# Batch 0's first quarter of q as fp32 on ScalarE's DMA queue, packed by heads and transposed in 128x128 blocks

## The chip, the cores and the metric

The kernel runs on one core of a Trainium2 chip. The time is the device time of one execution in microseconds (us). The kernel before took 399.16 us as the median of five runs (399.06 to 399.82). Beside these runs there is one profiled execution, from which all rows of a profile come.

A core has five engines, each with its own queue of instructions that it works through in order: TensorE (PE; its weight loads are shown as PEld), VectorE (DVE), ScalarE (ACT), GpSimd (POOL) and SyncE (SP). Transfers are issued from SP's and ACT's queues (the profile calls them hardware queues) and from POOL's (the software queue), and are carried by 16 DMA engines. Only transfers on POOL's queue change the type from fp32 to bf16 on the way here.

## The reference, cut to what matters

Attention with projected keys and values, then a feed-forward layer with a maximum over three matrices:

```python
k_proj = np.einsum('ks,bhsd->bhkd', E, k)       # E, F: 64 x 1024
v_proj = np.einsum('ks,bhsd->bhkd', F, v)       # q, k, v: 8 batches, 8 heads, 1024, 64
scores = scale * np.matmul(q, k_proj.transpose(0, 1, 3, 2))
attn = softmax(scores)                          # written out in the reference
x = np.matmul(attn, v_proj)                     # heads side by side: 8192 x 512
h = np.maximum(np.maximum(x @ w1, x @ w2), x @ w3)   # 512 x 768 each
out = h @ w_out                                 # 768 x 512
```

All inputs and the output are fp32; the kernel works in bf16 with fp32 sums.

## The kernel before, in words

The program works batch by batch, and each batch in two chunks of 512 rows. A row index s is split as s = p * 8 + si, with p the partition; a chunk is four of the eight si. For one chunk the up part (L687 and `up`, L738) multiplies x by the three weight matrices, 128 columns (jt, of six) at a time, and takes the maximum. The down part (L788) multiplies by w_out and stores. The attention of the next batch is put between these matmuls by a hand-written plan (L830 on). The instructions of each engine run in the order in which the program writes them; a small model of the clocks (`clock`, `free`, L67) only decides which of the eight PSUM banks a step takes, and `at(us)` (L588) sets that model's time by hand.

Batch 0 has a head of its own, L652 to L682, and this is where the change lies. Its transfers are all issued at the start:

- SP loads E and F (L148, L149) as fp32, 64 rows each, into `ef_f`.
- POOL loads, in this order: q for heads 0 to 3 and the first four si (`load_q(LO, ...)`, L167), k for heads 0 to 3 (L168), q for heads 4 to 7 and the first four si (L169), k for heads 4 to 7 (L170), two pieces of v (L171, L172), then after `ident` has been made weights, the two other pieces of v, more weights, the rest of q (L194) and w_out.

The head computes with the first chunk of q alone (`C0 = (0, SPC)`):

- `idle(n, w)` (L563) are filler matmuls on zeros; with `warm_f` in fp32, with `warm` in bf16.
- `turn_ef` (L570) casts E and F to bf16 (`ef_b`, half on DVE, half on ACT), transposes them in eight 128x128 blocks on TensorE (L578), and copies the result to `efT`, half on DVE, half on ACT.
- `q_duo(0)` (L633, with `heads_q`, L361) transposes q for two pairs of heads: 16 transposes of 64 columns each, since a head has 64 numbers and the heads of a pair lie apart in `q_t`; DVE copies the result to `qT`.
- A DVE copy (L656) writes the F columns of `efT` a second time.
- `k_duo(u)` (L593) projects k for four heads with `efT` (L596), `kt_duo(u)` transposes the result (L609), `scores` (L219) multiplies it with `qT`, `exps`, `z` and `x` make the softmax and the first x, `v_pair` (L622) projects v.
- `up_first` (L702) starts the first chunk's up matmuls (L689) while the later heads' attention is still under way. Its first maxima lie in `hs`, a fp32 tile of 128 x 6 x 512 that exists once; its first writes are the copies at L725.

For the second chunk of batch 0, `pack_q` (L373) copies q so that the two heads of a pair lie side by side (tile `q_p`), on ACT, and `qp` (L386) transposes whole 128x128 blocks of it (L393).

```python
copy("s", q_pk[b][:, g, lo:lo + nsi].rearrange("p si h d -> p h si d"),
     qkv[b][0][:, 2 * g:2 * g + 2, lo:lo + nsi], (), 0.58)
```

Every plain copy is recorded at the line of the helper `copy` (L102), so in the profile such rows are told apart by their tiles.

Of the kernel before, what the change touches and what calls it, by code (L numbers as in the profile page):

```python
# [8 lines left out]
FP32 = mybir.dt.float32  # L9
BF16 = mybir.dt.bfloat16  # L10
# [5 lines left out]
def kernel(  # L16
# [13 lines left out]
    nc = tc.nc  # L30

    B, H, S, D = q.shape
# [5 lines left out]
    P = 128  # L38
    HALF = 64
    SI = 8  # L40
    NCT = DM // P
    NJT = DF // P
    NPAIR = H // 2
    CHUNK = 512
    NCHUNK = S // CHUNK
    SPC = SI // NCHUNK
# [24 lines left out]
    def deal(ns):  # L71
        clock["pe"] = max(clock["pe"], *(free[n] for n in ns))
        for n in ns:
            assert free[n] < OPEN
            free[n] = OPEN

    def two():
        n = min(range(0, 8, 2), key=lambda n: max(free[n:n + 2]))
        deal((n, n + 1))
        return psum_t[:, n:n + 2, :], (n, n + 1)  # L80

    def bank():
        n = min(range(8), key=lambda n: free[n])
        deal((n,))
        return psum_t[:, n, :], (n,)

    def pe(dt, wait=0.0):
        clock["pe"] = max(clock["pe"], wait) + dt
        return clock["pe"]

    def runs(eng, ready, dt, ns=()):
        if eng in clock:
            clock[eng] = max(clock[eng], ready + 0.06) + dt
            for n in ns:
                free[n] = clock[eng]
            return clock[eng]
        return ready + dt
# [3 lines left out]
    def copy(eng, o, i, ns=(), dt=0.65):  # L101
        done = {  # L102
            "v": nc.vector.tensor_copy, "s": nc.scalar.copy, "g": nc.gpsimd.tensor_copy
        }[eng](out=o, in_=i)
        runs(eng, clock["pe"] if ns else 0.0, dt, ns)
        return done
# [10 lines left out]
    def view(src, b):  # L117
        return src[b].rearrange("h (p si) d -> p h si d", si=SI)


    ident = const.tile([P, P], BF16, name="ident")
# [9 lines left out]
    qkv, qTs, kpTs, vps, pTs, zis, xTs = {}, {}, {}, {}, {}, {}, {}  # L131
# [19 lines left out]
    def load_kv(i, heads):  # L151
        nc.gpsimd.dma_start(  # L152
            out=qkv[0][i][:, heads], in_=view((q, k, v)[i], 0)[:, heads]
        )

    def load_q(heads, sis):
        nc.gpsimd.dma_start(  # L157
            out=q_t[:, heads, sis], in_=view(q, 0)[:, heads, sis]
        )
# [4 lines left out]

    LO, HI, ALL = slice(0, H // 2), slice(H // 2, H), slice(0, H)
    V2, V3 = slice(4, 6), slice(6, 8)
    load_q(LO, slice(0, SPC))  # L167
    load_kv(1, LO)  # L168
    load_q(HI, slice(0, SPC))  # L169
    load_kv(1, HI)  # L170
# [56 lines left out]
    def exps(b, g, lo, nsi, sc):  # L227
        t, ns, ready = sc
        pTs[b, g, lo] = att.tile([P, 2, CHUNK], BF16, name="pT", bufs=6)[:, :, 0:nsi * HALF]
        nc.scalar.activation(out=pTs[b, g, lo], in_=t, func=AF.Exp, scale=scale)  # L230
        runs("s", ready, 0.17 + nsi * 0.107, ns)
# [14 lines left out]
    def sums(b, g, lo, nsi):  # L246
        return pair_mm(b, g, lo, nsi, lambda rows, hp: ones[rows])
# [48 lines left out]
    def invert(b, g, lo, nsi, z):  # L296
        t, ns, ready = z
        zl = att.tile([P, 2, CHUNK], FP32, name="zl", bufs=1)[:, :, 0:nsi * HALF]
        nc.scalar.activation(out=zl, in_=t, func=AF.Ln)  # L299
        runs("s", ready, 0.17 + nsi * 0.107, ns)  # L300
        if nsi == SI:
            zi = zi_all(b)[:, g]
        else:
            zi = att.tile([P, 2, CHUNK // 2], FP32, name="zi0", bufs=4)
        nc.scalar.activation(out=zi, in_=zl, func=AF.Exp, scale=-1.0)  # L305
        zis[b, g, lo] = zi, runs("s", ready, 0.17 + nsi * 0.107)

    def values(b, g, lo, nsi):
        if b not in xTs:
            xTs[b] = att.tile([P, NCT, SI, P], BF16, name="xT")  # L310
        return pair_mm(b, g, lo, nsi, lambda rows, hp: vps[b][rows, 2 * g + hp, :])

    def scale_x(b, g, lo, nsi, av):
        t, ns, ready = av
        zi, when = zis.pop((b, g, lo))
        nc.vector.tensor_tensor(  # L316
            out=xTs[b][:, g, lo:lo + nsi, :].rearrange("a (c s) p -> a c (s p)", c=2),
            in0=t, in1=zi, op=ALU.mult,
        )
        runs("v", max(ready, when), 0.17 + nsi * 0.13, ns)  # L320
# [3 lines left out]
    def run_later():  # L324
        for f in later:
            f()
        later.clear()
# [33 lines left out]
    def heads_q(b, g, sis, t):  # L361
        for i, si in enumerate(sis):
            for hp in range(2):
                nc.tensor.transpose(
                    out=t[hp * HALF:(hp + 1) * HALF, i * P:(i + 1) * P],
                    in_=qkv[b][0][:, 2 * g + hp, si, :],
                    identity=ident,
                )
        pe(0.08 * len(sis))

    q_pk = {}

    def pack_q(b, gs, lo, nsi):  # L373


        def f():
            if b not in q_pk:
                q_pk[b] = att.tile([P, NPAIR, SI, 2, D], BF16, name="q_p", bufs=1)
            for g in gs:
                copy(  # L380
                    "s", q_pk[b][:, g, lo:lo + nsi].rearrange("p si h d -> p h si d"),
                    qkv[b][0][:, 2 * g:2 * g + 2, lo:lo + nsi], (), 0.58,
                )
        return f

# [184 lines left out]
    def turn_ef():  # L570
        for i in range(2):
            cols = slice(i * S // 2, (i + 1) * S // 2)
            copy("vs"[i], ef_b[:, cols], ef_f[:, cols])
        t, ns = two()
        t = t.bitcast(BF16)[:, 0]
        src = ef_b.rearrange("k (p si) -> k p si", si=SI)
        for si in range(SI):
            nc.tensor.transpose(  # L578
                out=t[:, si * P:(si + 1) * P], in_=src[:, :, si], identity=ident
            )  # L580
        pe(0.6)
        for i in range(2):
            copy(
                "vs"[i], efT[:, 4 * i:4 * i + 4, 0:P],
                t[:, i * CHUNK:(i + 1) * CHUNK].rearrange("p (si x) -> p si x", x=P), ns,
            )

    def at(us):  # L588
        clock["pe"] = max(clock["pe"], us)
# [43 lines left out]
    def q_duo(u):  # L633
        t, ns = bank()
        t = t.bitcast(BF16)
        for gg in range(2):
            heads_q(0, 2 * u + gg, range(SPC), t[:, gg * CHUNK:(gg + 1) * CHUNK])
        o = qTs[0].rearrange("a (g si) p -> a g si p", si=SI)
        copy(
            "v", o[:, 2 * u:2 * u + 2, 0:SPC, :],  # L640
            t.rearrange("a (g si p) -> a g si p", si=SPC, p=P), ns, 0.7,
        )

    C0 = (0, SPC)

    def z(g):
        invert(0, g, *C0, sums(0, g, *C0))

    def x(g):
        scale_x(0, g, *C0, values(0, g, *C0))  # L650

    idle(3, warm_f)  # L652
    at(6.3)
    turn_ef()
    q_duo(0)
    copy("v", efT[:, :, P:P + KP], efT[:, :, KP:P])  # L656
    idle(1, warm_f)
    at(9.0)
# [4 lines left out]
    for g in (0, 1):  # L663
        exps(0, g, *C0, scores(0, g, *C0))
    at(10.6)
# [12 lines left out]
    for g in (2, 3):  # L678
        exps(0, g, *C0, scores(0, g, *C0))
    at(16.1)  # L680
    v_pair(1)
    at(17.4)  # L682

    ffn_sb = ctx.enter_context(tc.tile_pool(name="ffn_sb", bufs=2))
    hTs = {}

    def up_mm(h, i, b, ch, jt, cts, first=0, last=NCT - 1):  # L687
# [14 lines left out]
    def up_first(work):  # L702


        def then(key):
            run_later()
            for f in work.get(key, []):
                f()

        hs = ffn_sb.tile([P, NJT, CHUNK], FP32, name="hs", bufs=1)  # L710
        hTs[0, 0] = ffn_sb.tile([P, NJT, CHUNK], BF16, name="hT")
        jts = range(NJT)
        h = {}
        for ct, js in (
            (0, range(0, 4)), (1, range(0, 4)), (0, range(4, 6)), (1, range(4, 6)),
            (2, jts), (3, jts),
        ):
            for jt in js:
                if jt not in h:
                    t, ns = two()  # L720
                    for n in (0, 1):
                        h[jt + n] = t[:, n], ns[n:n + 1]
                up_mm(h[jt][0], 0, 0, 0, jt, (ct,))
                if ct == NCT - 1:
                    copy("sv"[jt % 2], hs[:, jt], *h[jt])  # L725
                then((0, ct, jt))
        for i in (1, 2):
            h = []
            for jt in jts:
                h.append(bank())  # L730
                up_mm(h[jt][0], i, 0, 0, jt, range(NCT // 2))
                then((i, "a", jt))
            for jt in jts:
                up_mm(h[jt][0], i, 0, 0, jt, range(NCT // 2, NCT))
                most(hs[:, jt] if i == 1 else hTs[0, 0][:, jt, :], *h[jt], hs[:, jt])
                then((i, jt))
# [154 lines left out]
    for b in range(B):  # L891
        p = plan(b)
# [63 lines left out]
```

## Time and profile before

| | |
|---|---|
| median of five runs | 399.16 us |
| profiled execution, its own time | 399.06 us |
| its span in the profile | 397.3 us |
| granted TensorE clock | 1.0 |
| DMA, mean over the span | 167 GB/s |
| POOL issues: first q quarter, first k half | at 1.26 and 2.14 us |
| issue to landing: E, F | 3.2 and 4.3 us |
| issue to landing: the two first quarters of q | 5.3 and 8.3 us |
| first k projection (L596), first matmul | 9.97 us |
| first up matmul (L689) | 17.65 us |

Times in the profile are counted from the start of the span. A row of the timeline gives the start, the duration, the engine, the line, the operation with the tile it writes and the tile it reads, and in brackets how long the engine was idle before it and what ended that idle time. "x8" behind a row means that eight instructions are merged. The view of the transfers counts packets, the pieces in which a queue moves its data, for each queue in a window, and gives the busy share of the 16 DMA engines, which may pass 1 where an engine has several pieces in flight. The page of the whole execution gives the busy time of each engine, and the chain of work that ended last, followed back from the end.

### The profile page before, as it was taken

What the parts mean: (1) busy time and instruction counts of PE and PEld (TensorE: products, weight loads), DVE (VectorE), ACT (ScalarE), POOL (GpSimd) and SP (SyncE); (2) the same over time, 40 slices, a digit from 0 to 9 for tenths busy, and PEclk for the clock granted to TensorE, in tenths of its full rate; (3) what the DMA queues carried; (4) which work ended last, traced back from release to release, by engine and by line L of the source; (5) the groups of instructions that cost most, each with busy time, mean ns of one, the idle gap of its engine ahead of it and who ended that gap; (6) DMA issues with size and microseconds to landing.
All of it is one profiled execution on the core that took longest, in us unless ns stands there. A gap on an engine that the chain in (4) does not pass through costs nothing.

```text
span 397.3 us, 5598 instructions
## 1 busy us (share of the span) xinstructions
PE 387.2 (97%) x2196; PEld 173.6 (44%) x2238; DVE 202.3 (51%) x309; ACT 152.1 (38%) x236; POOL 34.5 (9%) x49
## 2 busy tenths in 40 slices
PE   7999999999999999999999999999999999999996
PEld 3544443453445445444444444444444444444443
DVE  3348756751764525645374544845266443745251
ACT  2534638527222552263323532245323533132322
POOL 7440011000400200200002000200000000000000
PEclk9999999999999999999999999999999999999999
DMA  9999999987899998999979979696971138020202
GB/s 151 205 205 208 205 247 148 248 149 159 229 181 260 157 224 200 229 184 202 213 208 149 245 164 272 101 241 117 221 207 42 63 89 235 2 106 0 107 0 106
DMA packets 67338, 66.29 MB, mean 167 GB/s; under 512 B 31504, under 2 KB 59792, under 8 KB 67312
## 3 DMA queue, kind: packets, MB, share of 16 engines
q0 software_dynamic: 29104, 30.41, 47.4%
q1 hardware_dynamic: 38064, 35.46, 34.6%
q8 instruction: 17, 0.28, 0.3%
q10 hardware_dynamic: 144, 0.07, 0.1%
q14 instruction: 9, 0.07, 0.1%
HBM read 69.73 MB, written 16.97 MB: 218 GB/s over the span
## 4 chain that ended last, share of the span: by engine, by line
PE 90%; DMA 3%; DVE 2%; POOL 2%; issue 1%; ACT 1%; DVEq 0%; ACTq 0%; POOLq 0%
PE banks L689 61%; PE banks L797 20%; DMA v_t<-in_v_dram 3%; PE banks L239 2%; PE banks L353 2%; PE banks L219 2%; PE banks L528 1%; PE banks L264 1%; DVE xT L316 1%; DVE m L758 1%; ACT zi_all L305 1%; ACT zl L299 1%; DVE hT L699 0%; POOL k_t L152 0%; POOL q_t L157 0%
## 5 line engine op out<-in xcount | busy, mean ns | idle before, releaser
L689 PE MATMUL banks<-xT,w_sb 128*128 128x512 bf16 x1125 | 255.2, 379 | 1.9 <-DVE xT L316 0.3
L689 PEld LDWEIGHTS <-w_sb 128*128 128x128 bf16 x1152 | 110.2, 98 | 136.7 <-issue 8.5
L758 DVE TENSOR_TENSOR m<-banks,h1s 128x512 f32<-128x512 f32 x90 | 62.1, 690 | 131.3 <-ACT h1s L754 88.6
L754 ACT COPY h1s<-banks 128x512 f32<-128x512 f32 x90 | 52.7, 586 | 119.5 <-PE banks L689 119.5
L797 PE MATMUL banks<-wout_sb,hT 128*128 128x512 bf16 x364 | 85.5, 380 | 1.0 <-issue 0.3
L699 DVE TENSOR_TENSOR hT<-banks,m 128x512 bf16<-128x512 f32 x90 | 62.3, 692 | 9.7 <-DVE m L758 0.5
L797 PEld LDWEIGHTS <-hT 128*128 128x128 bf16 x378 | 35.3, 98 | 48.3 <-issue 6.1
L102 ACT COPY o_sb<-banks 128x512 f32<-128x512 f32 (+2 forms) x57 | 32.9, 578 | 58.3 <-PE banks L797 50.6
L316 DVE TENSOR_TENSOR xT<-banks,zi_all 128x1024 bf16<-128x1024 f32 x28 | 33.2, 1220 | 12.8 <-PE banks L239 8.2
L230 ACT ACTIVATE pT<-banks 128x1024 bf16<-128x1024 f32 (+1 forms) x32 | 30.3, 976 | 16.0 <-PE banks L219 16.0
L201 POOL DMA_DIRECT2D q_t<-in_q_dram x7 | 6.1, 877 | 196.7 <-DMA qT<-q_p 60.7
L102 ACT CAST vp<-banks 64x256 bf16<-64x256 f32 (+1 forms) x11 | 4.7, 424 | 20.5 <-DVE kp L102 11.2
L102 DVE CAST vp<-banks 64x256 bf16<-64x256 f32 (+2 forms) x15 | 6.7, 445 | 10.1 <-ACT vp L102 7.3
L239 PE MATMUL banks<-pT,vp 64*64 64x512 bf16 (+1 forms) x128 | 10.3, 375 | 0.5 <-DVE vp L102 0.2
L102 DVE COPY q_p<-q_t 128x1024 bf16<-128x1024 bf16 x26 | 9.7, 433 | 0.2 <-DMA q_t<-in_q_dram 0.2
L219 PE MATMUL banks<-qT,kpT 64*64 64x512 bf16 (+1 forms) x128 | 9.7, 372 | 0.0
L102 DVE CAST kp<-banks 128x256 bf16<-128x256 f32 (+2 forms) x9 | 4.6, 509 | 8.7 <-PE banks L528 3.5
L102 DVE COPY o_sb<-banks 128x512 f32<-128x512 f32 (+1 forms) x9 | 5.6, 640 | 5.4 <-PE banks L777 4.5
L567 PE MATMUL banks<-warm_f 128*128 128x512 f32 x8 | 6.4, 946 | 1.5 <-DVE warm_f L175 1.5
L299 ACT ACTIVATE zl<-banks 128x512 f32<-128x512 f32 (+1 forms) x8 | 6.5, 811 | 2.9 <-PE banks L239 2.7
L353 PEld LDWEIGHTS <-efT 128*64 128x64 bf16 x128 | 6.6, 110 | 2.1 <-issue 2.1
L201 POOL DMA_DIRECT2D v_t<-in_v_dram x7 | 6.5, 931 | 1.0 <-PE banks L689 1.0
(76 smaller groups left out, 136.3 us busy)
## 6 DMA issues: line engine op xcount, KB each, us to landing
out_dram<-o_sb SPq DMA_DIRECT2D x30, 512.0 KB, 3.8
zi_all<-zd SPq DMA_DIRECT2D x20, 512.0 KB, 7.9
q_t<-in_q_dram POOLq DMA_DIRECT2D x7, 1024.0 KB, 10.7
k_t<-in_k_dram POOLq DMA_DIRECT2D x7, 1024.0 KB, 17.1
v_t<-in_v_dram POOLq DMA_DIRECT2D x7, 1024.0 KB, 21.6
zi_all<-zd POOLq DMA_DIRECT2D x4, 512.0 KB, 7.6
w_sb<-in_moe_w_dram POOLq DMA_DIRECT2D x4, 384.0 KB, 11.1
k_t<-in_k_dram POOLq DMA_DIRECT2D x2, 512.0 KB, 9.0
```

Of the source, the lines that this page charges most:

```text
L102: done = {"v": nc.vector.tensor_copy, "s": nc.scalar.copy, "g": nc.gpsimd.tensor_copy}[eng](out=o, in_=i)
L201: dma = nc.gpsimd.dma_start(out=tiles[i], in_=view((q, k, v)[i], b))
L219: nc.tensor.matmul(out=t[c * HALF:(c + 1) * HALF, hp, 0:n * P], lhsT=k_pair(b, g)[rows], rhs=qTs[b][rows, at:at + n, :], start=True, stop= ...
L230: nc.scalar.activation(out=pTs[b, g, lo], in_=t, func=AF.Exp, scale=scale)
L239: nc.tensor.matmul(out=t[hp * HALF:(hp + 1) * HALF, c, 0:nsi * HALF], lhsT=w(rows, hp), rhs=p[rows, hp, :], start=True, stop=True,)
L316: nc.vector.tensor_tensor(out=xTs[b][:, g, lo:lo + nsi, :].rearrange("a (c s) p -> a c (s p)", c=2), in0=t, in1=zi, op=ALU.mult,)
L353: nc.tensor.matmul(out=t[hh * HALF:(hh + 1) * HALF, 0:width], lhsT=efT[:, si, (kv - 1) * KP:kv * KP], rhs=qkv[b][kv][:, heads[hh], si, :], ...
L689: nc.tensor.matmul(out=h, lhsT=w_sb[i][:, ct, jt * P:(jt + 1) * P], rhs=xTs[b][:, ct, ch * SPC:(ch + 1) * SPC, :], start=(ct == first), st ...
L699: nc.vector.tensor_tensor(out=o, in0=h, in1=other, op=ALU.max)
L754: nc.scalar.copy(out=h1s, in_=h[0][0])
L758: nc.vector.tensor_tensor(out=m12, in0=h[1][0], in1=h1s, op=ALU.max)
L797: nc.tensor.matmul(out=o_ps, lhsT=hTs[b, ch][:, jt, tt * P:(tt + 1) * P], rhs=wout_sb[:, jt, :], start=(jt == 0), stop=(jt == NJT - 1),)
```

## The change

The q quarter of heads 0 to 3 and the first four si leaves POOL's queue. It is loaded on ACT's queue, as fp32 without a change of type, into the first two of the six parts of `hs`; for this the pool of `hs` is opened earlier and `hs` is allocated in the head. The DMA stands ahead of ACT's table load (L174) in the program. Right behind the two casts of E and F, `pack_q` casts and packs this quarter by pairs of heads into `q_p`: pair 0 on DVE, pair 1 on ACT. In place of `q_duo(0)`, a new `q_first` transposes eight 128x128 blocks of `q_p`, and DVE copies the result to `qT`. The second quarter (heads 4 to 7) still comes over POOL and is still turned by `q_duo(1)`.

```diff
     LO, HI, ALL = slice(0, H // 2), slice(H // 2, H), slice(0, H)
     V2, V3 = slice(4, 6), slice(6, 8)
-    load_q(LO, slice(0, SPC))
+    ffn_sb = ctx.enter_context(tc.tile_pool(name="ffn_sb", bufs=2))
+    hs = ffn_sb.tile([P, NJT, CHUNK], FP32, name="hs", bufs=1)
+    q_f = hs[:, 0:2].rearrange("p j f -> p (j f)").rearrange(
+        "p (h si d) -> p h si d", h=H // 2, d=D
+    )
+    nc.scalar.dma_start(out=q_f, in_=view(q, 0)[:, LO, 0:SPC])
     load_kv(1, LO)
...
-    def pack_q(b, gs, lo, nsi):
+    def pack_q(b, gs, lo, nsi, engs="ss", src=None):
...
-            for g in gs:
+            for g, eng in zip(gs, engs):
+                i = qkv[b][0][:, :, lo:lo + nsi] if src is None else src
                 copy(
-                    "s", q_pk[b][:, g, lo:lo + nsi].rearrange("p si h d -> p h si d"),
-                    qkv[b][0][:, 2 * g:2 * g + 2, lo:lo + nsi], (), 0.58,
+                    eng, q_pk[b][:, g, lo:lo + nsi].rearrange("p si h d -> p h si d"),
+                    i[:, 2 * g:2 * g + 2], (), 0.58,
                 )
...
             copy("vs"[i], ef_b[:, cols], ef_f[:, cols])
+        pack_q(0, (0, 1), 0, SPC, "vs", q_f)()
         t, ns = two()
...
+    def q_first():
+        t, ns = bank()
+        t = t.bitcast(BF16)
+        for gg in range(2):
+            for si in range(SPC):
+                n = gg * SPC + si
+                nc.tensor.transpose(
+                    out=t[:, n * P:(n + 1) * P],
+                    in_=q_pk[0][:, gg, si].rearrange("p h d -> p (h d)"),
+                    identity=ident,
+                )
+        pe(0.5)
+        o = qTs[0].rearrange("a (g si) p -> a g si p", si=SI)
+        copy(
+            "v", o[:, 0:2, 0:SPC, :],
+            t.rearrange("a (g si p) -> a g si p", si=SPC, p=P), ns, 0.7,
+        )
...
     turn_ef()
-    q_duo(0)
+    q_first()
     copy("v", efT[:, :, P:P + KP], efT[:, :, KP:P])
...
-    ffn_sb = ctx.enter_context(tc.tile_pool(name="ffn_sb", bufs=2))
     hTs = {}
...
-        hs = ffn_sb.tile([P, NJT, CHUNK], FP32, name="hs", bufs=1)
         hTs[0, 0] = ffn_sb.tile([P, NJT, CHUNK], BF16, name="hT")
```

## The prediction

> **What bounds the kernel now.** I read the page's busy table first, then the chain that ended last, then the start of the timeline, because the change touches only the first 10 us.
>
> ```profile
> PE 387.2 (97%) x2196; PEld 173.6 (44%) x2238; DVE 202.3 (51%) x309; ACT 152.1 (38%) x236; POOL 34.5 (9%) x49
> ```
>
> TensorE is busy 97% of the span, so an edit in the head pays only if the moment shifts from which TensorE never waits again. The timeline from 16 to 40 us shows that moment:
>
> ```profile
> 17.61 0.13 PEld L689 LDWEIGHTS <-w_sb 128*128 128x128 bf16 x2 [0.31 <-DMA w_sb<-in_moe_w_dram]
> 17.65 0.59 PE L689 MATMUL banks<-xT,w_sb 128*128 128x512 bf16 x2 [0.17 <-DVE xT L316]
> ...
> 20.34 0.62 PE L622 MATMUL banks<-v_t,efT 128*128 128x128 bf16 x8 [0.17 <-DMA v_t<-in_v_dram]
> ...
> 23.81 9.29 PE L689 MATMUL banks<-xT,w_sb 128*128 128x512 bf16 x41
> ```
>
> From 23.81 TensorE is dense. Before it, transfers and a chain of dependent steps arrive within 0.2 to 0.3 us of each other: at 17.6 the weights (0.31) and xT (0.17) are both late. So an early gain reaches the end only if both move: the transfers, and the chain that starts at k_duo(0) (L596). The timeline from 0 to 16 us shows what starts that chain:
>
> ```profile
> 1.26 0.89 POOL L157 DMA_DIRECT2D q_t<-in_q_dram  x1 [0.81 <-POOLq L940]
> ...
> 5.74 0.55 DVE L102 CAST ef_b<-ef_f 128x512 bf16<-128x512 f32 x1 [3.50 <-DMA ef_f<-in_F_dram]
> ...
> 7.79 0.69 DVE L102 COPY qT<-banks 128x1024 bf16<-128x1024 bf16 x1
> 8.40 0.28 DVE L102 COPY efT<-efT 128x512 bf16<-128x512 bf16 x1
> 8.74 0.11 PEld L596 LDWEIGHTS <-efT 128*64 128x64 bf16 x1 [0.76 <-DVE efT L102]
> 9.97 1.03 PE L596 MATMUL banks<-k_t,efT 128*64 128x256 bf16 x8 [1.16 <-DMA k_t<-in_k_dram]
> ```
>
> efT is ready at 8.74, the first half of k only at 9.97. The q quarter, first on POOL's queue, had no reader waiting for it, but it stands ahead of that k.
>
> **POOL and the stream.** One issue of 0.89 us goes, so POOL issues k at 1.26 instead of 2.14. Its later issues wait for earlier landings (the last v piece of the head is issued at 10.21, after 2.0 us of waiting for k_t), so they move with the landings, not by 0.89. The bytes decide. In the window 5.0 to 5.5 us, 179 pieces of the q quarter (512 bytes written, 1 KB read) went through 16 engines: 0.5 x 16 / 179 = 0.045 us each; 512 pieces are 32 per engine, 1.43 us. The same 512 pieces now come over ScalarE's queue with 1 KB written. No fp32 load in such pieces is in the trace; from both sides: the last stores (512 bytes to 2 KB) ran at 278 to 396 GB/s, so 512 KB are 1.3 to 1.9 us. I take 0.045 us a piece, which lies between. So the work stays the same, and the stream gains only what q does before POOL's data starts. POOL's data starts late, as the windows of half a microsecond show (columns: four engines' busy time, POOL, clock, DMA share, GB/s):
>
> ```profile
> 2.50:3.00 0.50, 0.50 (x2) 0.31 (x1) 0.00 (x0) 0.00 (x0) 0.50 (x2) 1.00 0.93 262
> 3.00:3.50 0.50, 0.50 (x2) 0.18 (x1) 0.00 (x0) 0.00 (x0) 0.50 (x1) 1.00 1.95 263
> 3.50:4.00 0.50, 0.50 (x2) 0.16 (x1) 0.00 (x0) 0.00 (x0) 0.50 (x2) 1.00 0.35 48
> 4.00:4.50 0.50, 0.50 (x2) 0.32 (x1) 0.00 (x0) 0.00 (x0) 0.50 (x2) 1.00 0.83 219
> ```
>
> E and F run from 2.1, POOL's pieces in numbers only after 4.0 (54 packets in 4.0 to 4.5, 144 in the next half), and 65% of 3.5 to 4.0 is idle.
>
> A rule speaks against the change: the Trainium skill, "DMA: Bandwidth & Descriptors", section "Issuing engines are not separate DMA queues", says that DMAs of all issuers run on the same 16 engines, so a second issuer only saves issuing time. By it alone the stream would gain nothing and the time would stay at 399.1. The 0.35 above says that here there is idle time to fill. The same page's "Latency and other measured facts" gives first bytes after about 1 us (POOL) and 0.6 us (hardware queue), which would shrink that idle time by over a microsecond; the trace shows 2.8 us from POOL's first issue to its data at 4.1 and 1.3 us for E, and I go by the trace.
>
> **When q lands.** How queues share an engine shows from 120 to 122 us, with transposes on SP's queue beside loads on POOL's:
>
> ```profile
> q0 software_dynamic: 307, 0.31, 92.1%
> q1 hardware_dynamic: 307, 0.08, 29.7%
> ```
>
> Piece for piece, one to one, whatever the size. So beside the 8 pieces of 4 KB per engine of E and F, q gets 8 of its 32 through, plus about 9 in the idle parts (0.33 us of 3.5 to 4.0, 0.08 of 4.0 to 4.5, at 0.045): 17 by 4.3. The other 15 alternate with k's pieces (84 in 6.0 to 6.5: 0.5 x 16 / 84 = 0.095 us each): 15 x (0.045 + 0.095) = 2.1, so q's last data at 6.4. F's data ended about 4.9 and F landed at 1.37 + 4.3 = 5.67; with 0.8 for that tail **q lands at about 7.2**. Ends: no idle time used, 24 pieces left at 4.4, 4.4 + 3.4 + 0.8 = 8.5; all of E, F and q at 400 GB/s before POOL's data, 2.1 + 2.6 + 0.8 = 5.5.
>
> **The new wait.** Two casts wait for q: one on DVE (0.55, row of ef_b), one on ACT (0.62, its ACT twin). ACT is idle from its table load to 5.72, which hides its DMA issue (SP's E issue took 0.58). Behind DVE's cast stand the efT copy, the qT copy and the efT doubling, behind ACT's the other half of efT; k_duo(0) waits for the doubling. From q's landing: ACT cast 0.65 with its start, 0.06 to TensorE. The 8 transposes of 128x128 take what L578's 8 take, 0.66, against 0.64 for today's 16: nothing gained. The old q transposes began at 7.11; the doubling let L596 load at 8.74 (1.63 later), the filler matmul of warm_f ended at 8.80 (1.69 later). So k_duo(0) can start at landing + 0.65 + 0.06 + 1.69 = landing + 2.40: **9.6** with q at 7.2. If q lands by 6.6 to 6.7 the casts hide beside the ef transposes (6.53 to 7.2) and cost nothing; then F is next, 8 x 0.045 = 0.36 late, k_duo(0) at 9.1 to 9.2.
>
> k itself: 17 pieces x 0.045 = 0.76 us of q's work lie ahead of POOL's data, so k lands about 0.7 sooner, 9.3, and k halves, v and weights behind it as much. q is thus the later of the two, at 9.6: a new wait in place of the old. The chain moves by 9.97 - 9.6 = 0.37, the stream by 0.7; the smaller counts at 17.6.
>
> **Costed at nothing.** The pool opened earlier and the shared buffer: hs is first written at 25.16, q is read out before 9. The later packs keep ACT and their place (31.81). The 0.1 us of planner time that differ are swallowed by the set times. If batch 1's loads move 0.7 earlier, they only land earlier.
>
> **The sum.** In the profiled execution (399.06, span 397.3, so 1.76 around it) 399.06 - 0.37 = 398.7. The median of the five runs is 0.1 higher: **398.8**.
>
> **Rivals.**
> 1. The chain gains all it can: q lands before 6.7, k_duo(0) at 9.1 to 9.2 and the stream 0.8 to 0.9 sooner: 0.8 to 0.9 off, plus up to 0.2 from the transfer waits at 17.6 and 20.3: 398.2 (397.9 to 398.4). For it: the idle share of 0.35. Against it: q's pieces get only every second turn.
> 2. Slower: q loses the turns. The one-to-one sharing leaves 24 pieces beside k, q lands at 8.5 and k_duo(0) starts at 10.9, 0.93 late; the stream's gain can't be used, since the chain comes last at 17.6: 400.1 (399.4 to 400.3). It decides from a landing at 9.97 - 2.40 = 7.57. For it: the turns, and F's slow end (5.67) today. Against it: engines idle before 4.1.
> 3. It moves bytes without an effect: q's work before 4.1 only delays E and F, and k lands where it did: 399.1.
>
> **Chances.** Forecast 0.38 (398.8, from 398.4 to 399.1), rival 1 0.30, rival 2 0.27, rival 3 0.05. A measurement can tell about 0.2%, 0.8 us, from no change: faster is below 398.36, slower above 399.96. Faster: 0.26 of rival 1 and 0.04 of the forecast's low end, 0.30. Slower: 0.25 of rival 2. The rest, 0.45, within. The range takes rival 1's low end and rival 2's high end: 397.9 to 400.3.
>
> **What would show it.** In the changed profile: ACT's first work is a DMA issue at 0.73; k's issue at 1.26 on POOL; POOL's data still starts near 4.1; the q transfer lands at 7.2 by the two casts' wait; L596's first matmul at 9.6 with the wait put to efT or the casts, not to k_t; L689 at 17.2. If L596 still waits for k_t, the stream did not move; if the casts start at 6.3 right behind ef_b, rival 1 holds; if L596 starts after 10, rival 2. A k_t landing no earlier than 9.97 would mean that POOL's data is limited by something other than the engines' time, and my working of the stream is wrong.

## The result and the profile after

The changed kernel takes 400.26 us (median of 31 runs, 398.79 to 402.90) beside 399.27 us before (57 runs, 398.45 to 400.12): a ratio of 1.0021, 95% interval 1.0013 to 1.0028. The ratios follow the means of the runs rather than the medians. The kernel is a little slower, where the prediction had 398.8. The profiled execution took 400.79 us; its span is 399.0, against 397.3 before.

The page's list of the lines on the last chain is where I looked first: the list of the kernel before, then the two rows of the changed one.

```profile
PE banks L689 61%; PE banks L797 20%; DMA v_t<-in_v_dram 3%; PE banks L239 2%; PE banks L353 2%; PE banks L219 2%; PE banks L528 1%; PE banks L264 1%; DVE xT L316 1%; DVE m L758 1%; ACT zi_all L305 1%; ACT zl L299 1%; DVE hT L699 0%; POOL k_t L152 0%; POOL q_t L157 0%
...
PE 92%; DVE 3%; DMA 2%; ACT 1%; issue 1%; SPq 0%; DVEq 0%; ACTq 0%
PE banks L713 61%; PE banks L820 19%; PE banks L244 2%; PE banks L224 2%; PE banks L358 2%; DMA ef_f<-in_F_dram 2%; PE banks L534 1%; DVE xT L321 1%; PE banks L573 1%; PE banks L269 1%; DVE m L781 1%; PE banks L603 1%; ACT zi_all L310 1%; ACT zl L304 1%; DVE hT L723 0%
```

Before, the transfer on that chain was v's: the chain ran over POOL's issues to v's landing at 20.3. Now it is F's; no transfer of q, k or v stands in the list. The timeline of the changed kernel (start, duration, engine, line; in brackets the idle time before and its releaser) shows what F's lateness does. L585 is the old L578, L603 the old L596, L713 the old L689.

```profile
0.74 0.57 SPq L148 DMA_DIRECT2D ef_f<-in_E_dram  x1
0.74 0.45 ACTq L172 DMA_DIRECT2D hs<-in_q_dram  x1
...
7.77 0.62 ACT L102 CAST ef_b<-ef_f 128x512 bf16<-128x512 f32 x1 [5.26 <-DMA ef_f<-in_F_dram]
8.13 0.42 DVE L102 CAST q_p<-hs 128x512 bf16<-128x512 f32 x1
...
8.45 0.70 PE L585 MATMUL banks<-ident,ef_b 128*128 128x128 bf16 x8 [1.99 <-ACT ef_b L102]
8.98 0.81 PE L657 MATMUL banks<-ident,q_p 128*128 128x128 bf16 x8
9.59 2.02 PE L573 MATMUL banks<-warm_f 128*128 128x512 f32 x2
...
11.54 1.59 PE L603 MATMUL banks<-k_t,efT 128*64 128x256 bf16 x8
...
19.77 0.59 PE L713 MATMUL banks<-xT,w_sb 128*128 128x512 bf16 x2 [0.17 <-DVE xT L321]
```

- The casts of E and F begin at 7.77, where they began at 5.72 before. The cast of q follows at once and waits for nothing: q had landed at 0.74 + 4.8 = 5.54 by the table of issues, F at 1.36 + 6.3 = 7.69.
- TensorE has nothing to do from 6.46 to 8.45.
- The same two filler matmuls of `warm_f` take 2.02 us instead of 1.12, and the eight k projections 1.59 instead of 1.03. So they run at a lower clock. The first up matmul starts 2.12 us later than before (19.77 against 17.65), and the dense stretch 1.8 later.

Windows of the same kernel show the clock (busy time of PE, PEld, DVE, ACT and POOL, then the granted clock, DMA share, GB/s).

```profile
8.00:9.00 1.00, 0.56 (x9) 0.56 (x10) 0.55 (x2) 0.91 (x2) 0.00 (x0) 1.00 1.19 176
9.00:10.00 1.00, 1.00 (x12) 1.00 (x11) 0.59 (x2) 0.35 (x1) 0.17 (x1) 0.62 1.33 187
10.00:12.00 2.00, 2.00 (x5) 0.42 (x5) 0.72 (x2) 0.23 (x1) 1.09 (x2) 0.50 1.25 203
12.00:14.00 2.00, 2.00 (x12) 1.07 (x10) 0.51 (x2) 0.00 (x0) 0.15 (x1) 0.84 1.24 205
```

Full clock to 9, half from about 9.3 to 12.7, full again: some 3.4 us at half speed, begun 2.8 us after TensorE fell idle and 0.8 us after it had work again.

The windows from 2.0 to 4.0 us answer to those shown of before: 387 and 391 GB/s instead of 262 and 263, and the idle time between 3.5 and 4.0 is gone.

```profile
2.50:3.00 0.50, 0.50 (x2) 0.31 (x1) 0.00 (x0) 0.01 (x1) 0.50 (x2) 1.00 1.09 387
3.00:3.50 0.50, 0.50 (x2) 0.17 (x1) 0.00 (x0) 0.00 (x0) 0.50 (x1) 1.00 1.08 391
3.50:4.00 0.50, 0.50 (x2) 0.16 (x1) 0.00 (x0) 0.00 (x0) 0.50 (x2) 1.00 1.03 330
```

Who fills them is in the DMA view of the changed kernel from 2 to 3 us. q10 is ScalarE's queue, q1 is SP's, q0 is POOL's:

```profile
q10 hardware_dynamic: 332, 0.34, 98.1%
```

This is q and nothing else: E, issued at the same 0.74, moves its first pieces only between 3.0 and 3.5 (17 of them). Before, the same microsecond held 72 pieces of SP's queue at 83.2%.

The 32 listed runs of the changed kernel (one, of 402.05, is not among the 31 of the median) fall into two groups by their mean granted clock: 14 with 0.998 or more took 398.79 to 399.87 (median 399.17, as before), 18 with 0.991 to 0.996 took 400.20 to 402.90 (median 400.73). 3.4 us at half clock are 1.7 / 399 = 0.4% of the span, which makes a mean of 0.996. So the groups look like runs without and with the stretch that the windows show.

### The profile page after: what moved, and what is told of

It reads as the page before. It is cut to its first block, busy times and chain, and to the rows that moved or that the text cites. A ratio compares the mean times of both kernels' runs of the same rounds, so it can differ in the third digit from the quotient of the medians.

```text
span 399.0 us, 5585 instructions
## 1 busy us (share of the span) xinstructions
PE 388.3 (97%) x2188; PEld 174.2 (44%) x2230; DVE 202.6 (51%) x310; ACT 152.5 (38%) x237; POOL 33.4 (8%) x48
## 4 chain that ended last, share of the span: by engine, by line
PE 92%; DVE 3%; DMA 2%; ACT 1%; issue 1%; SPq 0%; DVEq 0%; ACTq 0%
PE banks L713 61%; PE banks L820 19%; PE banks L244 2%; PE banks L224 2%; PE banks L358 2%; DMA ef_f<-in_F_dram 2%; PE banks L534 1%; DVE xT L321 1%; PE banks L573 1%; PE banks L269 1%; DVE m L781 1%; PE banks L603 1%; ACT zi_all L310 1%; ACT zl L304 1%; DVE hT L723 0%
## 5 line engine op out<-in xcount | busy, mean ns | idle before, releaser
L713 PE MATMUL banks<-xT,w_sb 128*128 128x512 bf16 x1125 | 255.2, 379 | 1.9 <-DVE xT L321 0.3
L713 PEld LDWEIGHTS <-w_sb 128*128 128x128 bf16 x1152 | 110.2, 98 | 136.7 <-issue 8.8
L102 ACT CAST vp<-banks 64x256 bf16<-64x256 f32 (+1 forms) x11 | 4.7, 424 | 20.5 <-DVE kp L102 11.2
```

Source lines behind the costliest of these rows:

```text
L102: done = {"v": nc.vector.tensor_copy, "s": nc.scalar.copy, "g": nc.gpsimd.tensor_copy}[eng](out=o, in_=i)
L713: nc.tensor.matmul(out=h, lhsT=w_sb[i][:, ct, jt * P:(jt + 1) * P], rhs=xTs[b][:, ct, ch * SPC:(ch + 1) * SPC, :], start=(ct == first), st ...
```

## The experiments

**Theory.** q's transfer goes ahead of E's and F's. F lands 2 us late, TensorE's filler work ends before that, and the hole of 2 us costs the full clock for 3.4 us. The price is the clock, not the 2 us. **Rivals:** the lateness of F itself is the price, with or without the clock; or the packing, the casts or the shared buffer cost something.

### Is the price the clock?

**Filler over the hole** (changed kernel, one more fp32 filler ahead of `turn_ef`):

```diff
-    idle(3, warm_f)
+    idle(4, warm_f)
```

> The changed kernel with four fp32 fillers in place of three at the head, so that TensorE stays busy to about 8.1 us while E and F are awaited. Theory (the granted clock is the price): the clock stays at 1.0 from 9 to 14 us, the filler behind q_first takes 1.1 us instead of 2.0 and the first k projection 1.0 instead of 1.6, so the first up matmul comes at about 18.3 instead of 19.8, and all runs end near 399.1, within 0.2 of the kernel before. Rival (the late landing of F is the price, the clock only goes along with it): nothing but the hole is filled and the time stays near 400.3, spread from 398.8 to 401.

Measured: 399.01 us, ratio 1.0000 (0.9992 to 1.0009), every listed run with a clock of 0.998 or more. Its timeline:

```profile
7.37 0.62 ACT L102 CAST ef_b<-ef_f 128x512 bf16<-128x512 f32 x1 [4.88 <-DMA ef_f<-in_F_dram]
...
8.04 0.71 PE L585 MATMUL banks<-ident,ef_b 128*128 128x128 bf16 x8 [0.47 <-ACT ef_b L102]
...
9.03 1.08 PE L573 MATMUL banks<-warm_f 128*128 128x512 f32 x2
...
10.04 1.06 PE L603 MATMUL banks<-k_t,efT 128*64 128x256 bf16 x8
...
17.75 0.59 PE L713 MATMUL banks<-xT,w_sb 128*128 128x512 bf16 x2 [0.17 <-DVE xT L321]
```

F is still 1.6 us later than before (7.28 against 5.67), the hole is 0.47, the clock stays at 1.00, and the first up matmul comes at 17.75, only 0.1 later than before. So an F at 7.28 costs next to nothing by itself: it uses up the 1.16 us for which L596 waited for k, and the steps from the cast to L603 take 2.67 us, where before they took 3.09 without that wait. From this run to the changed kernel's profile the 2.02 us at the first up matmul are F's further 0.40, 1.10 between the cast and L603 (0.94 of it the filler), and 0.53 in L603.

**The hole alone, in the kernel before** (its filler behind `q_duo(0)` taken out, nothing of the change):

```diff
     q_duo(0)
-    idle(1, warm_f)
```

> The kernel before without the one fp32 filler matmul behind q_duo(0), so that TensorE is idle from about 7.8 to 9.97 us, 2.2 us, as long as the hole in the profile of the changed kernel; no transfer is touched. Theory (an idle TensorE of about 2 us costs granted clock for the next microseconds): the clock falls below 0.8 between 9 and 13 us in most runs, the first k projection takes 1.3 to 1.6 us instead of 1.03, and the time rises by 0.5 to 1.5: 399.6 to 400.6. Rival (the clock falls for another reason, such as the late casts): clock 1.0 and 399.1.

Measured: 399.93 us, ratio 1.0022 (1.0011 to 1.0032), the same as the whole change. Its windows:

```profile
10.00:12.00 2.00, 1.90 (x9) 1.29 (x9) 0.00 (x0) 0.00 (x0) 0.99 (x2) 0.52 1.26 199
12.00:14.00 2.00, 2.00 (x15) 0.47 (x17) 0.64 (x2) 0.05 (x1) 0.27 (x1) 0.62 1.25 206
```

The idle time is 2.17 us from 7.94; k lands no later in any way that matters (L596 at 10.11, 0.14 late), yet L596 takes 1.87 instead of 1.03, and the first up matmul starts at 19.18, 1.5 late. Three of the seven runs list a mean clock of 0.995 or 0.996, four 0.999 or 1.000 (399.04 to 400.17). Two of the runs (399.04 and 399.29) lost nothing that can be told with the same filler missing; what divides the runs, how long the hole is in each or when it falls, is not shown.

**A longer hole** (changed kernel, one filler fewer):

```diff
-    idle(3, warm_f)
+    idle(2, warm_f)
```

> The changed kernel with two fp32 fillers at the head instead of three, so that TensorE's hole ahead of the ef transposes grows by about 1.7 us in every run, to 3 us or more; no transfer is touched. Theory (the two groups of runs of the changed kernel are those with a shorter and a longer hole): all runs lose clock (mean 0.992 to 0.996), none is below 400, median 400.6 to 401.5. Rival (the groups come from the transfers, the clock only goes along): the two groups stay, some runs near 399.1.

Measured: 401.67 us, ratio 1.0063 (1.0050 to 1.0077), no run below 401. In its profile TensorE idles 3.77 us (4.85 to 8.62) and the clock is 0.50 from about 7.8 to 14.5, twice as long as in the changed kernel. One thing stays open: three of its five runs (401.42 to 401.70) list a mean clock of 0.999 or 1.000. The listed mean may miss a stretch, so a listed 1.0 is no proof that the clock held. For the same reason the two groups above support the theory and don't prove it; it rests on the two runs before this one.

The Trainium skill, "TensorE: Matmul & The Clock Gate", "Part 1: The HAM clock gate", says that TensorE falls to half rate after an idle window of about 3.4 us, and that this window runs free instead of starting with the kernel. The half rate agrees with the 0.50 here. The idle time needed does not: holes of 1.99, 2.17 and (queues exchanged, below) 2.42 us were enough in these profiles, while 1.63 (POOL's stream later, below), 1.16 in the kernel before and 0.47 left the clock at 1.00. A free-running window would fit that the clock fell 2.0 us after TensorE became idle in one profile and 5.1 in another; no run here tests it.

### Why did F land late?

**q behind E and F** (changed kernel):

```diff
-    nc.scalar.dma_start(out=q_f, in_=view(q, 0)[:, LO, 0:SPC])
+    nc.sync.dma_start(out=q_f, in_=view(q, 0)[:, LO, 0:SPC])
```

> The changed kernel with q's fp32 load on SP's queue, behind E and F, all else the same. Theory (q's 512 pieces go first and push E and F back): F lands at 5.7 to 6.0 instead of 7.7, ef_b is cast at about 6, q lands at 7 to 8, the hole on TensorE is under 1.2 us, the clock stays at 1.0, the first k projection starts at 9.6 to 10.3: 399.0 to 399.6. Rival (the bytes themselves delay, in whatever order): E and F or q land near 7.7 all the same and the time stays at 400.3.

Measured: 404.11 us, ratio 1.0128 (1.0115 to 1.0141). F lands at 5.37, so q ahead of it had indeed been its hindrance. But q, issued at 2.00, moves next to nothing before 6 and lands at 11.3. POOL's stream had begun by then, and from 7 to 8 us the two queues move nearly equal numbers of pieces:

```profile
q0 software_dynamic: 142, 0.11, 66.8%
q1 hardware_dynamic: 140, 0.14, 50.7%
```

Its timeline shows the new wait, with a hole of 4.91 us on TensorE and a half clock behind it:

```profile
11.28 0.62 ACT L102 CAST q_p<-hs 128x512 bf16<-128x512 f32 x1 [5.18 <-DMA hs<-in_q_dram]
...
11.77 1.02 PE L657 MATMUL banks<-ident,q_p 128*128 128x128 bf16 x8 [4.91 <-DVE q_p L102]
...
14.53 1.38 PE L603 MATMUL banks<-k_t,efT 128*64 128x256 bf16 x8
```

This is the second rival of the prediction, larger than it was priced there.

**The queues exchanged** (changed kernel; q alone on SP's queue, E and F on ScalarE's):

```diff
-    nc.sync.dma_start(out=ef_f[0:KP], in_=E)
-    nc.sync.dma_start(out=ef_f[KP:P], in_=F)
+    nc.scalar.dma_start(out=ef_f[0:KP], in_=E)
+    nc.scalar.dma_start(out=ef_f[KP:P], in_=F)
...
-    nc.scalar.dma_start(out=q_f, in_=view(q, 0)[:, LO, 0:SPC])
+    nc.sync.dma_start(out=q_f, in_=view(q, 0)[:, LO, 0:SPC])
```

> The changed kernel with the two hardware queues swapped: q alone on SP's queue, E and F one behind the other on ACT's. Theory A (ACT's transfer is begun ahead of SP's when both are issued at 0.74): E's pieces start at 2.1 and q's only at about 3, F behind; E lands near 4, F at 5.7 to 6.5, the clock is kept more often: 398.6 to 399.6. Theory B (the transfer of many small pieces goes ahead, on whichever queue): q's pieces again start at 2.1 and E's after 3, F lands at 7.3 to 7.7, and the runs fall into the same two groups, median near 400.

Measured: 400.34 us, ratio 1.0033 (1.0018 to 1.0048). From 2 to 3 us again only q moves, now on SP's queue (q1):

```profile
q1 hardware_dynamic: 201, 0.21, 63.6%
```

F lands at 7.43. Which queue carries q makes no difference: the transfer of 512 pieces of 1 KB starts ahead of the one of 4 KB pieces issued beside it. Why it does, these runs don't show. TensorE was idle for 2.42 us from 5.72, and the clock was 0.50 from 7.8 to 11.2.

**POOL's stream 0.65 us later** (changed kernel, e9 in a later text; `ident` and three clears made on POOL ahead of its first load, so that k is issued at 1.89 instead of 1.24):

```diff
+    make_identity(nc, ident)
+    nc.gpsimd.memset(warm, 0.0)
+    nc.gpsimd.memset(ones, 1.0)
+    nc.gpsimd.memset(pick, 0.0)
...
-    nc.vector.memset(warm, 0.0)
-    make_identity(nc, ident)
-    nc.vector.memset(ones, 1.0)
-    nc.vector.memset(pick, 0.0)
```

> The changed kernel with POOL's first load (k) issued about 1 us later, behind the identity matrix and three memsets that POOL now makes first. Theory A (q ahead of E and F is the whole delay of F): F lands at 7.3 to 7.7 as before, the clock falls in about half of the runs, median 399 to 400.7, and k is later too. Theory B (F's last pieces take turns with POOL's pieces, which is most of the delay): F lands 0.7 to 1 us earlier, at 6.3 to 6.8, no hole above 1 us, clock 1.0 in all runs: 398.6 to 399.3.

Measured: 399.30 us, ratio 1.0017 (1.0002 to 1.0032); 8 of 12 runs list a clock of 0.998 or more (398.52 to 399.84), 4 a lower one (400.76 to 401.65). F lands at 7.06 instead of 7.69. But the profile is of the fastest run (398.52, hole of 1.63 us, clock 1.00 throughout), and in the profiles with one filler more and one fewer, whose transfers are those of the changed kernel, F landed at 7.28 and 7.86. So turns with POOL's pieces may make 0.2 to 0.8 us of F's lateness; these profiles don't settle it. The other 1.4 us are there with POOL later too. POOL's issue that waits for k's first half came at 9.43, earlier than the 9.83 of the changed kernel, though k was issued 0.65 later.

**F on ScalarE's queue ahead of q** (changed kernel; e3 in the texts that follow):

```diff
-    nc.sync.dma_start(out=ef_f[KP:P], in_=F)
+    nc.scalar.dma_start(out=ef_f[KP:P], in_=F)
```

> The changed kernel with F on ACT's queue ahead of q, E alone on SP's: E and F start together, q behind F. Theory (order decides): E and F land by 5.0 to 5.7, q by 6.5 to 7.5, the first k projection at 9.1 to 9.9, k about 0.4 earlier than before the change: 398.4 to 399.1. Rival (the two hardware queues are served one after the other, ACT's first): E, alone on SP, lands last, after 7, and the time is near 400.3.

Measured: 403.28 us, ratio 1.0082 (1.0052 to 1.0112), in two groups: 3 runs of 398.51 to 399.26, 9 of 402.18 to 404.12 (clock 0.991 to 0.995). The profile is of the short kind: F at 4.44, E at 5.54, q at 7.05, L603 at 9.31. To see the long kind I moved the making of `ident` ahead of POOL's loads as well (e6; k issued at 1.43, 0.2 later and not the 0.65 that the text expected):

```diff
+    make_identity(nc, ident)
...
-    nc.sync.dma_start(out=ef_f[KP:P], in_=F)
+    nc.scalar.dma_start(out=ef_f[KP:P], in_=F)
...
-    make_identity(nc, ident)
```

> The kernel of e3 (F on ACT's queue ahead of q), with the identity matrix made on POOL ahead of its loads, so that POOL's first load (k) is issued some 0.65 us later, after q's issue on ACT. Theory (transfers issued in the first microseconds start one behind the other; in e3's long runs q's issue lost the race against k's and q waited behind k's data): q is ahead of k in every run, all runs are like e3's short ones, 398.3 to 399.3 with clock 1.0, median 398.7. Rival (e3's long runs come from something else, such as F and q sharing ACT's queue): the two groups near 398.6 and 403.4 stay.

Measured: 399.11 us, ratio 1.0024 (0.9999 to 1.0049), 7 runs of 398.47 to 399.23 and 5 of 400.87 to 403.19. Its profile is a long one: q's last pieces trickle beside POOL's (20 in 6.0 to 6.5, then 12, 10, 7, 5, 3 per half microsecond), q lands at 9.97, TensorE idles 3.95 us (6.57 to 10.52) and the clock is 0.50 from 11.7 to 15.0. With POOL delayed by 0.65 us, the two edits joined:

```diff
+    make_identity(nc, ident)
+    nc.gpsimd.memset(warm, 0.0)
+    nc.gpsimd.memset(ones, 1.0)
+    nc.gpsimd.memset(pick, 0.0)
...
-    nc.sync.dma_start(out=ef_f[KP:P], in_=F)
+    nc.scalar.dma_start(out=ef_f[KP:P], in_=F)
...
-    nc.vector.memset(warm, 0.0)
-    make_identity(nc, ident)
-    nc.vector.memset(ones, 1.0)
-    nc.vector.memset(pick, 0.0)
```

> The kernel of e3 (F on ACT's queue ahead of q) with POOL's first load about 1 us later, as in e9; in e6 it came only 0.2 later, since POOL's start was the bound. Theory (the long runs are those in which the end of q's transfer takes turns with POOL's pieces): q lands by 7.2 in every run, the first k projection starts at 9.2 to 9.9, clock 1.0, all runs 398.3 to 399.3. Rival (something else makes q's end late): long runs above 400.8 stay, as in e6 (5 of 12).

Measured: 399.27 us, ratio 1.0007 (0.9999 to 1.0016), no long run in 11. The profiles and this run fit one reading: a run is long where q is not through when POOL's pieces come. No long run without the moved `ident` was profiled.

The three profiles show one thing more. E and F, here issued together on the two queues and alike in size, were not shared evenly either: from 2 to 3 us 46 pieces of F and none of E moved in the first, 63 of E and one of F in the second, 36 of E and none of F in the third. So one transfer goes first even where the two are alike, and it is not always the same queue's.

In the last of them the chain is as early as the prediction hoped for, and yet nothing is gained; the timeline shows why:

```profile
9.28 1.03 PE L604 MATMUL banks<-k_t,efT 128*64 128x256 bf16 x8
...
16.96 0.59 PE L714 MATMUL banks<-xT,w_sb 128*128 128x512 bf16 x2 [0.17 <-DVE xT L322]
...
20.21 0.62 PE L630 MATMUL banks<-v_t,efT 128*128 128x128 bf16 x8 [0.71 <-DMA v_t<-in_v_dram]
```

The first up matmul is 0.69 earlier than before, then TensorE waits 0.71 for v, which lands when it landed before (the wait ended at 20.34 there, at 20.21 here; in the profile of e3, where POOL is not delayed, at 20.24 after 0.72). What sets that moment is not shown. It is not the bytes alone: in the profile with POOL's stream later the same v matmuls (L630) began at 19.91 and waited for no transfer, with all bytes moved.

### Packing, and less of q

**The packing alone** (kernel before, q over POOL in bf16 as before, but packed by `pack_q` on DVE and ACT and turned by `q_first`):

```diff
+        pack_q(0, (0, 1), 0, SPC, "vs")()
...
-    q_duo(0)
+    q_first()
```

> The kernel before with only the packing and the 128x128 transposes: the first q quarter still comes over POOL as bf16 and is packed from q_t, half on DVE and half on ACT. Theory (the packing is hidden behind the wait for k): q lands at about 6.6, the casts end at about 7.2, the efT doubling ends by 9.0, the first k projection still starts at 9.97 behind k_t: 399.2 to 399.4, no change. Rival (the casts and the longer chain are the price): the first k projection starts after 10.2 and the time is 399.6 or more.

Measured: 399.52 us, ratio 1.0008 (0.9998 to 1.0018): no difference that can be told. In its profile the efT doubling ends at 9.07, and L603 still waits 1.04 us for k, to 10.10. The wait for k hides the packing.

**One head of four over ScalarE** (changed kernel; heads 1 to 3 of the quarter are not loaded but filled with a constant, so a part of the input is left out):

```diff
-    nc.scalar.dma_start(out=q_f, in_=view(q, 0)[:, LO, 0:SPC])
+    nc.scalar.dma_start(out=q_f[:, 0:1], in_=view(q, 0)[:, 0:1, 0:SPC])
+    nc.vector.memset(q_f[:, 1:4], 0.1)
```

> The changed kernel with only one of the four heads of the first q quarter loaded over ACT's queue (128 pieces instead of 512); heads 1 to 3 of it are filled with a constant by VectorE, so that part of the output is left out. Theory (the number of q's pieces ahead of E and F sets when F lands): F lands at about 6.0 to 6.3 instead of 7.3 to 7.7, TensorE's hole stays under 0.6 us, clock 1.0, the first k projection starts behind k near 9.0 to 9.5: 398.3 to 399.0. Rival (any transfer on ACT's queue, whatever its size, delays E and F by its latency): F lands after 7, the clock drops in about half of the runs as with the changed kernel.

Measured: 398.52 us, ratio 0.9991 (0.9982 to 0.9999). F lands at 6.76, TensorE's matmuls no longer wait for v, and the first up matmul is at 17.46. Even with 384 KB of fp32 q not moved at all the gain is 0.1%. The fill also moved the fillers 0.8 us later, which closed the hole, so this run does not price the transfer by itself.

**Half over ScalarE, half over POOL** (heads 2 and 3 first on POOL's queue):

```diff
-    nc.scalar.dma_start(out=q_f, in_=view(q, 0)[:, LO, 0:SPC])
+    nc.scalar.dma_start(out=q_f[:, 0:2], in_=view(q, 0)[:, 0:2, 0:SPC])
+    load_q(slice(2, 4), slice(0, SPC))
...
-        pack_q(0, (0, 1), 0, SPC, "vs", q_f)()
+        pack_q(0, (0,), 0, SPC, "v", q_f)()
+        pack_q(0, (1,), 0, SPC, "s")()
```

> The changed kernel with q's first quarter split: heads 0 and 1 (256 pieces) as fp32 over ACT's queue, heads 2 and 3 first on POOL's queue as before the change and packed from q_t on ACT. An attempt at a version better than both. Theory (pieces ahead of E and F set F's landing and with it the hole): F lands at 6.8 to 7.1, the hole is about 1 us, the clock stays at 1.0 in most runs, the first k projection starts at 9.6 to 9.9, the stream is about 0.4 earlier: 398.6 to 399.0. Rival (half the pieces delay F as much as all): F after 7.3, the clock falls in about half of the runs, median 399.5 to 400.5.

Measured: 399.65 us, ratio 1.0018 (1.0004 to 1.0032). F lands at 6.58, the hole is 1.00 in the profile, and 4 of 12 runs list a clock of 0.994 to 0.996. It is no better than the kernel before. No version that computes everything beat it clear of the noise. In two profiles with an earlier chain, v was the next to wait for; where the chain was earlier and v in time (POOL's stream later, 398.52 in its profile), the runs with a listed clock of 0.998 or more had a median of 399.05, against 399.06 before.

## Why the prediction was wrong

The direction was wrong, and two steps failed.

1. **"beside the 8 pieces of 4 KB per engine of E and F, q gets 8 of its 32 through"**. I took the equal numbers of pieces from 120 to 122 us, where both queues were in full flow, for two transfers that start together. Here q went first and alone (332 pieces from 2 to 3 us, none of E). So q landed at 5.54. That this is the low end of my bounds (5.5) is luck: that bound had E and F through by then too, but E landed at 5.84 and F at 7.69. The delay fell on F. The prediction priced that at "8 x 0.045 = 0.36 late"; it was 2.0 (1.6 in the profile with the hole filled). The exchanged queues show that this lies in the two transfers and not in the queue.
2. **The sum had no term for the clock.** I looked at the granted clock, saw 1.00 in all the windows that I showed, and worked on as if it were fixed. The fillers of `warm_f` were in the rows that I read, and I never asked how long TensorE may wait before the clock falls. Those fillers end at 6.46 in the changed kernel: the 2 us that follow without work were paid for by 3.4 us at half speed in the profile. Filling the hole brought the ratio to 1.0000, and making the same hole in the kernel before brought it to 1.0022, against 1.0021 for the change. Within their intervals these two runs account for the whole difference, though not for which executions lose the clock.

Beside these:

- **The stream** was to come 0.7 us earlier. POOL's v issue, which waits for k's first half, starts at 9.83 instead of 10.21, so 0.4 in the changed kernel; with the hole filled and the same transfers it was 10.15, only 0.06. So these profiles show no sure gain of the stream.
- **"k_duo(0) can start at landing + 2.40"** was nearly right where q was the last to come: 7.05 to 9.31, 2.26, with F on ScalarE's queue. In the changed kernel itself q was not what was waited for.
- **"The smaller counts"** held in two profiles. The chain was 0.7 early there and gained nothing, since v came no earlier (0.71 and 0.72 of wait). Rival 1's 398.2 was not reached even with q and F both in time (399.27).
- **Rival 2**, q losing the turns, is real and dear (1.0128 with q behind E and F on SP's queue), but its condition, q landing after 7.57, did not come about in the changed kernel. Its 400.1 lies near the measured 400.26 by luck: the slower time came by a way that I had not listed. (Its sum 4.4 + 3.4 + 0.8 makes 8.6, not 8.5; nothing hangs on that.)
- **Rival 3**, to which I gave 0.05, came nearest to what the transfers did: q delays E and F, and k lands nearly where it did (0.06 to 0.4 earlier). Its 399.1 is what the changed kernel takes with the hole filled (399.01). It lacked the price of the idle TensorE too.
- **Costed at nothing**: the packing and the two casts are hidden (1.0008, interval through 1.0; the cast of q follows that of F at once), and no run showed a cost of the shared buffer.

## What to carry to other kernels

Filler matmuls are cut to a certain wait; when a change moves the landing for which they fill, price the idle time on TensorE as well as the delay: here a hole of 2 us cost another 1.5 us behind it, at half clock, in the runs that lost the clock. When a transfer is moved to a queue that looked free, ask what moves in the same microsecond and which of the two goes first, since a transfer for which nobody waits can delay the one that everything waits for. And an earlier chain is worth what the next transfer on its way allows, which the timeline shows some rows further down.

## What the runs showed of the hardware

- Two transfers issued together on the two hardware queues were not shared evenly at first. 512 pieces of 1 KB went alone for a microsecond, on either queue, ahead of 64 pieces of 4 KB; of two transfers of 64 such pieces, now the one and now the other went first. Beside POOL's stream, a hardware queue moved as many pieces as POOL's from 7 to 9 us in one profile (140 and 142 in one microsecond), but the last pieces of q in another came at 12 beside 88 of POOL's in half a microsecond.
- POOL's first pieces came when the first hardware transfers were nearly through: in numbers from about 4.1 us before, from about 5 in the changed kernel, from about 6 with F on ScalarE's queue (with k issued at 1.25 as at 1.89; from about 5.5 in the profile with k at 1.43). A hardware transfer issued at 2.00 behind E and F got next to nothing until about 6, after POOL's pieces had begun.
- The granted clock fell to 0.50 some 2.0 to 2.9 us after TensorE became idle in four profiles (idle from 5.72, 7.94, 6.46 and 4.85; half clock from about 7.8, 10.1, 9.3 and 7.8), also where it had work again by then. In the two where q landed late (11.3 and 9.97) it fell only 5.0 and 5.1 us after (idle from 6.86 and 6.57; half clock from about 11.9 and 11.7). It stayed at half for 3.4 us in five of these six, after holes of 2.0 to 4.9 us, and for 6.8 after one of 3.8. So the length of the hole alone told neither when the clock fell nor for how long.
